# Half of wq on 120 partitions: two hardware loads of the query weights become pieces on GpSimd's queue, ScalarE's queue and SP's queue

## The chip, the cores and the metric

The kernel runs on one core of one Trainium2 chip. The metric is the device time of one execution in microseconds (us), taken as a median over runs. Before the change it is 1324.21 us (three runs, 1323.97 to 1324.29).

## What is computed

The reference is one decode step for two batch rows: a pre-LayerNorm attention block over a long cache, then an MLP. B = 2, D = 512, H = 32 heads of DH = 128, a cache of SK = 8192 positions, all in float32.

```python
h  = x + attention(layernorm(x))
h2 = h + mlp(layernorm(h))            # 512 -> 1792 -> 512, with gelu

def attention(x):
    q = (x @ wq).reshape(B, 1, H, DH)                 # wq: 512 x 4096
    scores = einsum("bhqd,bhkd->bhqk", q, k_cache) * DH ** -0.5
    o = einsum("bhqk,bhkd->bhqd", softmax(scores), v_cache)
    return o.reshape(B, 1, H * DH) @ wo
```

The two caches are 64 tiles each of 8192 x 128 floats, 4 MB (4096 KB in the profile) a tile; together they are nearly all of the 561 MB that the kernel reads. wq is 8 MB.

## The kernel before

**Tiles.** One pair (head h, batch row b) has one key tile and one value tile, 128 partitions of 32 KB. The 64 pairs run in order of h, then b. All these tiles, the two tiles of wq at the start and the MLP weights at the end rotate through one pool, `kv`, of five buffers (`BUFS = 5`, L42). A second pool, `wts`, has two buffers for the 1 MB groups of wo (`load_wo`, L55). A load is issued on SP's queue (`nc.sync.dma_start`) and waits there, ahead of all later loads, until the buffer that it takes is free.

**Start.** x comes in on ScalarE's queue (L49). wq comes in as two tiles of 4 MB on SP's queue (L61 to L66): partition p holds the rows 4p to 4p+3 of wq, two of them in each tile. VectorE and ScalarE compute the layer norm of x (L100 to L109; the Sqrt on ScalarE at L105 is `lnsd`), TensorE transposes it row group by row group (L113, tile `ypt`, copied to `yT` at L115), and 32 matrix instructions (L124) multiply it with wq, into the accumulators `so2`. ScalarE copies the sums to `q2` (L128), and `make_q` (L132) spreads two heads' worth of q over 128 partitions (`qps`, L136).

**Loop.** For pair i (L265), in two halves c of 32 positions per partition: VectorE multiplies the key tile with q in place (`multiply`, L161), sums most of the products (`by_dve`, L170) while ScalarE sums ten positions of each half (`by_act`, L166), takes the maximum over the row (`row_max`, L177), and with both batch rows of a head done the softmax follows (`all_max`, L184; `exps`, L194). The value tile of pair i-2 is multiplied on TensorE (`values`, L215). A key tile is free when VectorE and ScalarE are through with it, a value tile when TensorE is. I write k0, k1, ... and v0, v1, ... for the key and value tiles of pairs 0, 1, ...

**Order.** The loop asks at pair i for the key tile of pair i+1 and then the value tile of pair i-1 (L270, L278); the wo groups come at every eighth pair (L271) and the biases b1 and b2 at pair 56 (L279). The framework's scheduler then fixes the order in each queue, and it gives each DMA of the hardware queues (SP's and ScalarE's together) one of eight completion semaphores in turn; a DMA that takes a semaphore again waits until the DMA before it on that semaphore has landed. GpSimd's DMAs have eight semaphores of their own, used in the same way.

**End.** The last value tile comes in three pieces (L314), then w1 and w2 in ten pieces (L315 to L321). The MLP follows, and the output leaves on two queues (L420).

Of the kernel before, what the change touches and what calls it, by code (L numbers as in the profile page):

```python
# [9 lines left out]
F32 = mybir.dt.float32  # L10
BF16 = mybir.dt.bfloat16
AF = mybir.ActivationFunctionType
ALU = mybir.AluOpType
AX = mybir.AxisListType

P = 128
# [11 lines left out]
def tile_decode_block(ctx: ExitStack, tc: tile.TileContext, x, k, v, wq, wo, w1, b1, w2, b2, out):  # L28
    nc = tc.nc
    B, H, SK, DH = k.shape  # L30
    D = x.shape[-1]
# [3 lines left out]
    DC = D // P  # L35
# [4 lines left out]
    const = ctx.enter_context(tc.tile_pool(name="const", bufs=1))  # L40
    wts = ctx.enter_context(tc.tile_pool(name="wts", bufs=2))
    kv = ctx.enter_context(tc.tile_pool(name="kv", bufs=BUFS))  # L42
    work = ctx.enter_context(tc.tile_pool(name="work", bufs=3))
    psq = ctx.enter_context(tc.tile_pool(name="psq", bufs=2, space=bass.MemoryType.PSUM))
    psm = ctx.enter_context(tc.tile_pool(name="psm", bufs=3, space=bass.MemoryType.PSUM))
    psa = ctx.enter_context(tc.tile_pool(name="psa", bufs=1, space=bass.MemoryType.PSUM))

    x2 = const.tile([B, D], F32, name="x2")
# [9 lines left out]
        nc.sync.dma_start(t, rows.rearrange("(h p) n -> p h n" if g == LG else "(p h) n -> p h n", p=P))  # L58
        wo_g[g] = t

    wqv = wq.rearrange("(p r) n -> p r n", r=DC)  # L61
    wqs = []
    for r in range(0, DC, 2):
        t = kv.tile([P, 2, H * DH], F32, name="wqs", tag="kv")
        nc.sync.dma_start(t, wqv[:, r:r + 2, :])  # L65
        wqs += [t[:, 0, :], t[:, 1, :]]  # L66

    ident = const.tile([P, P], F32, name="ident")
    make_identity(nc, ident)
    epst = const.tile([P, 1], F32, name="epst")  # L70
    nc.vector.memset(epst, EPS)
    eps2 = const.tile([P, 1], F32, name="eps2")
# [23 lines left out]
    so2 = [psa.tile([P, 512], F32, name=f"so{j}") for j in range(2)]  # L96
# [5 lines left out]
    mv = work.tile([B, 2], F32, name="lnmv")  # L102
# [2 lines left out]
    nc.scalar.activation(sd, mv[:, 1:2], AF.Sqrt, bias=epst[:B])  # L105
    rs = work.tile([B, 1], F32, name="lnrs")
    nc.vector.reciprocal(rs, sd)
    y2 = const.tile([B, D], F32, name="y2")
    nc.vector.tensor_scalar(y2, x2, mv[:, 0:1], rs, op0=ALU.subtract, op1=ALU.mult)  # L109

    ypt = psm.tile([P, DC, B], F32, name="sm")
    for r in range(DC):
        nc.tensor.transpose(ypt[:, r, :], y2.rearrange("b (p r) -> b r p", r=DC)[:, r, :], ident[:B, :B])  # L113
    yT = const.tile([P, DC, B], F32, name="yT")
    nc.vector.tensor_copy(yT, ypt)  # L115
    pick = const.tile([P, B, P], F32, name="pick")
    nc.vector.tensor_copy(pick, sel_all[:, :B, None].to_broadcast([P, B, P]))

    QW = H * DH // NG
    q2 = const.tile([P, QW], F32, name="q2")  # L120
    for r in range(DC):
        for j in range(QW // 512):
            for n in range(NG):
                nc.tensor.matmul(so2[j][32 * n:32 * n + B], yT[:, r, :],  # L124
                                 wqs[r][:, n * QW + j * 512:n * QW + (j + 1) * 512],
                                 start=(r == 0), stop=(r == DC - 1))
    for j in range(QW // 512):
        nc.scalar.activation(q2[:, j * 512:(j + 1) * 512], so2[j], AF.Copy)  # L128

# [135 lines left out]
    for i in range(NP):  # L265
        h, b = pairs[i]
# [94 lines left out]
    with behind(last):  # L361
        for n in range(NG):
            last = nc.tensor.matmul(po2[32 * n:32 * n + 32], ident[:B, :32], resb[:, n * P:(n + 1) * P],
                                    start=True, stop=False)
# [10 lines left out]
    for c in range(DC):  # L375
        last = nc.tensor.matmul(acc[:, c, :], wlc.rearrange("d (p c) -> d c p", c=DC)[:, c, :], OT[hl],
                                start=True, stop=True)
    with behind(last):
        for n in range(NG):
            nc.tensor.matmul(po2[32 * n:32 * n + B], OT[hl], wl[:, n * P:(n + 1) * P],  # L380
                             start=False, stop=False)
# [8 lines left out]
    for c in range(DC):  # L390
        for n in range(NG):
            last = nc.tensor.matmul(
                pf[32 * n:32 * n + B], cen[:, c, :], w1t[:, c, n * FN:(n + 1) * FN],
                start=(c == 0), stop=(c == DC - 1))
# [18 lines left out]
    for t in range(FT):  # L413
        for n in range(NG):
            nc.tensor.matmul(po2[32 * n:32 * n + B], fT[:, t, :B], w2t[:, t, n * P:(n + 1) * P],
                             start=False, stop=(t == FT - 1))
# [29 lines left out]
```

## Time and profile before

| | |
|---|---|
| median of three runs | 1324.21 us |
| the profiled execution | 1324.32 us |
| its span, first to last instruction | 1322.5 us |
| VectorE busy | 989.5 us, 75% of the span |
| TensorE matmuls busy | 530.4 us, 40% |
| ScalarE busy | 442.0 us, 33% |
| GpSimd busy | 1.3 us |
| read from HBM | 561.01 MB, 424 GB/s over the span |
| packets of SP's and ScalarE's data queues | 22300, 98.9% of 16 engines' span |
| instruction queues q8 and q14 | 23 packets, 0.38 MB and 29 packets, 0.24 MB |
| median from issue to landing, key tile and value tile | 42.9 us and 34.4 us |

How to read it: the core has 16 DMA engines, and a load of 128 partitions puts 8 partitions on each of them. The DMA share is the mean over the 16. A load counts as landed when all the engines it uses have added to its semaphore; the trace records each of these additions and each packet. "PEclk" is the clock that TensorE was granted, as a part of full speed. In the chain of waits DMA has 73% of the span, VectorE 18% and TensorE 7%.

### The profile page before, as it was taken

How to read it: one execution, taken by the hardware profiler on the slowest of the kernel's cores; microseconds unless marked ns; L12 is line 12 of the kernel's file. 1: busy time of each engine (PE TensorE's matmuls, PEld its weight loads, DVE VectorE, ACT ScalarE, POOL GpSimd, SP SyncE). 2: the span in 40 equal slices, each digit the busy share in tenths (PEclk: the TensorE clock that was granted, in tenths of full speed). 3: DMA queues.
4: the chain of work that ended last, by engine and by line, in shares of the span. 5: the costliest groups of instructions: out<-in, count | busy, mean ns of one | idle time of the engine just before them, and what ended most of it. 6: DMA issues, size and time to landing. Idle time of an engine off the chain costs nothing.

```text
span 1322.5 us, 9641 instructions
## 1 busy us (share of the span) xinstructions
PE 530.4 (40%) x2901; PEld 143.3 (11%) x2901; DVE 989.5 (75%) x459; ACT 442.0 (33%) x2763; POOL 1.3 (0%) x10
## 2 busy tenths in 40 slices
PE   4044234334244244434336244263343532444347
PEld 1011001101011011100101011010011100011013
DVE  1997877867877778868778778777778768687781
ACT  0433323324323324324323333323333333243241
POOL 0000000000000000000000000000000000000000
PEclk9566666666676676676676666676766766666668
DMA  9999999999999999999999999999999999999995
GB/s 412 427 429 429 436 431 429 427 432 434 432 428 430 434 431 431 430 429 432 434 429 431 431 432 430 433 429 432 430 431 432 431 431 428 432 429 431 428 424 216
DMA packets 22364, 561.64 MB, mean 425 GB/s; under 512 B 2452, under 2 KB 2468, under 8 KB 4136
## 3 DMA queue, kind: packets, MB, share of 16 engines
q1 hardware_dynamic: 22300, 561.02, 98.9%
q8 instruction: 23, 0.38, 0.1%
q14 instruction: 29, 0.24, 0.0%
q10 hardware_dynamic: 12, 0.01, 0.0%
HBM read 561.01 MB, written 0.00 MB: 424 GB/s over the span
## 4 chain that ended last, share of the span: by engine, by line
DMA 73%; DVE 18%; PE 7%; issue 1%; ACT 0%; SPq 0%; DVEq 0%
DMA kv<-in_A_k_cache_dram 51%; DMA kv<-in_A_v_cache_dram 19%; DVE kv L161 12%; PE so L215 6%; DVE s L170 5%; DMA w1s<-in_B_w_dram 3%; DMA w2s<-in_B_w_dram 1%; PE qps L136 1%; DVE gm L184 0%; ACT kv L166 0%; DVE orow L242 0%; ACT L194 0%; DVE mx L177 0%; SPq L152 0%; SPq L65 0%
## 5 line engine op out<-in xcount | busy, mean ns | idle before, releaser
L161 DVE TENSOR_TENSOR kv<-kv,qps 128x4096 f32<-128x4096 f32 x128 | 562.3, 4413 | 286.3 <-DMA kv<-in_A_k_cache_dram 286.3
L166 ACT ACTIVATE kv<-kv 128x128 f32<-128x128 f32 x1280 | 376.0, 295 | 687.0 <-DVE kv L161 670.9
L215 PE MATMUL so<-kv,pt 128*8 128x512 f32 x2048 | 374.2, 855 | 258.6 <-DMA kv<-in_A_v_cache_dram 256.2
L170 DVE TENSOR_REDUCE s<-kv 128x22 f32<-128x2816 f32 x128 | 390.9, 3075 | 0.1
L166 ACT ACTIVATION_READ_ACCUMULATOR kv<-kv 128x1 f32 x1280 | 238.7, 187 | 0.0
L215 PEld LDWEIGHTS so<-kv,pt 128*8 128x8 f32 x2048 | 63.3, 113 | 500.2 <-DMA kv<-in_A_v_cache_dram 249.8
L186 PE MATMUL sm<-gm,srow 1*128 1x2 f32 x64 | 18.1, 349 | 192.1 <-DVE gm L184 192.1
L136 PE MATMUL qps<-q,pick 2*128 2x256 f32 x64 | 30.8, 631 | 135.7 <-DVE kv L161 135.7
L222 ACT ACTIVATE ss<-so 128x512 f32<-128x512 f32 x32 | 19.1, 597 | 148.4 <-PE so L215 148.4
L180 PE MATMUL sm<-ident,mx 128*1 128x128 f32 x64 | 17.7, 276 | 66.4 <-DVE mx L177 61.3
L254 PE MATMUL rowacc<-wog,ot 128*2 128x512 f32 x56 | 38.5, 852 | 5.2 <-DVE ot L252 5.0
L186 PEld LDWEIGHTS sm<-gm,srow 1*128 1x128 f32 x64 | 15.5, 299 | 204.2 <-DVE gm L184 160.7
L203 PE MATMUL sm<-ones,ls 128*2 128x1 f32 x56 | 5.4, 165 | 76.2 <-ACT pt L194 76.2
L232 PE MATMUL sm<-ss,sel 128*2 128x128 f32 x224 | 29.0, 273 | 13.3 <-ACT ss L222 13.1
L136 PEld LDWEIGHTS qps<-q,pick 2*128 2x128 f32 x64 | 17.5, 299 | 142.2 <-DVE kv L161 138.5
L194 ACT ACTIVATE pt<-s,nb 128x64 f32<-128x64 f32 x64 | 21.7, 340 | 1.1
L232 PEld LDWEIGHTS sm<-ss,sel 128*2 128x2 f32 x224 | 16.7, 84 | 23.5 <-ACT ss L222 19.4
L177 DVE TENSOR_REDUCE mx<-s 128x1 f32<-128x64 f32 x64 | 14.1, 220 | 6.5 <-ACT kv L166 0.2
L180 PEld LDWEIGHTS sm<-ident,mx 128*1 128x1 f32 x64 | 5.1, 79 | 122.9 <-DVE mx L177 77.0
L124 PE MATMUL so<-wqs,yT 128*2 128x512 f32 x64 | 10.8, 834 | 11.4 <-DMA wqs<-in_A_wq_dram 11.4
L184 DVE TENSOR_REDUCE gm<-sm 1x2 f32<-1x256 f32 x32 | 12.8, 401 | 0.5 <-PE sm L180 0.5
L237 DVE TENSOR_TENSOR ot<-sm,rl 128x2 f32<-128x2 f32 x4 | 0.6, 156 | 15.4 <-PE sm L230 15.4
(85 smaller groups left out, 109.6 us busy)
## 6 DMA issues: line engine op xcount, KB each, us to landing
kv<-in_A_k_cache_dram SPq DMA_DIRECT2D x63, 4096.0 KB, 42.9
kv<-in_A_v_cache_dram SPq DMA_DIRECT2D x62, 4096.0 KB, 34.4
wqs<-in_A_wq_dram SPq DMA_DIRECT2D x2, 4096.0 KB, 16.7
wog<-in_A_wo_dram SPq DMA_DIRECT2D x8, 1024.0 KB, 45.3
kv<-in_A_v_cache_dram SPq DMA_DIRECT2D x3, 2048.0 KB
kv<-in_A_k_cache_dram SPq DMA_DIRECT2D x2, 2048.0 KB, 40.1
w1s<-in_B_w_dram SPq DMA_DIRECT2D x4, 896.0 KB, 34.1
w2s<-in_B_w_dram SPq DMA_DIRECT2D x2, 1024.0 KB
```

What stands on the lines that cost most here:

```text
L136: nc.tensor.matmul(t[:, b], pick[32 * n:32 * n + B, b, :], q2[32 * n:32 * n + B, at:at + QG * DH], start=True, stop=True)
L161: return nc.vector.tensor_tensor(kc, kc, qb, op=ALU.mult)
L166: nc.scalar.activation(kt[:, j, :], kt[:, j, :], AF.Copy, accum_out=s[:, j:j + 1])
L170: nc.vector.tensor_reduce(ST[i][:, a:e], kt[:, a:e, :], axis=AX.X, op=ALU.add)
L177: nc.vector.tensor_reduce(MX[h][:, b:b + 1], ST[i], axis=AX.X, op=ALU.max)
L180: nc.tensor.transpose(MT[h][:, e, :], MX[h][:, e:e + 1], ident)
L186: nc.tensor.matmul(GM[h], srow, gm, start=True, stop=True)
L194: nc.scalar.activation(ptz[h % 2][b][:, :, 4 * b:4 * b + 4], s.rearrange("p (u j) -> p u j", j=4), AF.Exp, bias=nb[:, b:b + 1], scale=SCAL ...
L215: m = nc.tensor.matmul(so[32 * n:32 * n + 4 * B], ptz[h % 2][b][:, u, :], vt[:, 4 * u:4 * u + 4, :], start=(b == 0 and u < NG), stop=(b == ...
L222: nc.scalar.activation(SS[h], so2[h % 2], AF.Copy)
L232: nc.tensor.matmul(OP[h], sel[:, :, j], sj, start=(j == 0), stop=(j == 3))
L254: nc.tensor.matmul(rowacc, t[:, r, :], wo_g[g][:, r, :], start=(g == 0 and r == 0), stop=False)
```

## The change

wq has 512 rows. Rows 0 to 239 go into one tile, `wqa`, two rows to a partition, on 120 partitions; partitions 4 to 7 and 36 to 39 stay zero. Rows 240 to 495 go into a second tile, `wqb`, two rows on each of 128 partitions, in one load on SP's queue. The last 16 rows go on every eighth partition of two tiles of half a row each, `wqc`, which take the two buffers of the wo pool.

`wqa` comes in by 24 DMAs on GpSimd's queue and 8 on ScalarE's. On GpSimd's queue eight groups follow each other, their order held by `issue_after`: a filler of 2 elements of b1, a piece of 6 rows of 32 KB to partitions with a stride of 4, and a piece of 8 rows likewise. The 8 DMAs on ScalarE's queue carry one partition of 32 KB each, to partitions 0 to 3 and 32 to 35; they stand ahead of the Sqrt of the layer norm there.

VectorE and GpSimd first zero half of partitions 0 to 39 of `wqa` each (40 x 4096 elements), and VectorE zeroes both `wqc` tiles (128 x 2048 each). The DMAs into these tiles wait for that. The layer norm's result is written in five pieces instead of one, into a zeroed tile with gaps at the eight empty partitions; there are five transposes instead of four. The matrix instructions go over `wqb`, then `wqa`, then `wqc`: 16, 16 and 8 instead of 32.

In the order that the scheduler makes of it, on SP's queue: b2 (one row), `wqb`, the two `wqc`, k0, k1, k2, b1 (twice), b2, v0, k3, the first two wo groups, v1, k4, v2, k5, v3, and on as before. Before it is: the two wq tiles, k0, k1, k2, v0, k3, v1, k4, the first wo group, v2, k5, v3. b1 and b2 were loaded at pair 56.

```diff
--- before.py
+++ after.py
@@ -58,15 +58,48 @@
         nc.sync.dma_start(t, rows.rearrange("(h p) n -> p h n" if g == LG else "(p h) n -> p h n", p=P))
         wo_g[g] = t
 
-    wqv = wq.rearrange("(p r) n -> p r n", r=DC)
-    wqs = []
-    for r in range(0, DC, 2):
-        t = kv.tile([P, 2, H * DH], F32, name="wqs", tag="kv")
-        nc.sync.dma_start(t, wqv[:, r:r + 2, :])
-        wqs += [t[:, 0, :], t[:, 1, :]]
-
+
+
+    VOID = (4, 36)
+    NA = 2 * (P - 4 * len(VOID))
+    wqa = kv.tile([P, 2, H * DH], F32, name="wqs", tag="kv")
+    nc.vector.memset(wqa[0:40, 0], 0.0)
+    nc.gpsimd.memset(wqa[0:40, 1], 0.0)
     ident = const.tile([P, P], F32, name="ident")
     make_identity(nc, ident)
+    fill = const.tile([2, 8], F32, name="fill")
+    turns = iter(range(8))
+    rows = wq[0:NA].rearrange("(q r) n -> q r n", r=2)
+
+    pool = nc.gpsimd.memset(fill, 0.0)
+
+    def in_turn(dst, src):
+        nonlocal pool
+        with tc.issue_after(pool.ins):
+            pool = nc.gpsimd.dma_start(dst, src)
+
+    def turn_to(n):
+        e = next(turns)
+        in_turn(fill[:n, e:e + 1], b1[:, None][:n])
+
+    def spread(p0, q0, n):
+        in_turn(wqa[p0:p0 + 4 * n - 3:4], rows[q0:q0 + 4 * n - 3:4])
+
+    for half in range(2):
+        for j in range(4):
+            turn_to(2)
+            spread(32 * half + 8 + j, 28 * half + 4 + j, 6)
+            spread(64 + 32 * half + j, 56 + 32 * half + j, 8)
+    for half in range(2):
+        for j in range(4):
+            nc.scalar.dma_start(wqa[32 * half + j:32 * half + j + 1], rows[28 * half + j:28 * half + j + 1])
+    wqb = kv.tile([P, 2, H * DH], F32, name="wqs", tag="kv")
+    nc.sync.dma_start(wqb, wq[NA:NA + 2 * P].rearrange("(p r) n -> p r n", r=2))
+    wqc = [wts.tile([P, H * DH // 2], F32, name="wqc", tag="wog") for _ in range(2)]
+    for j in range(2):
+        nc.vector.memset(wqc[j], 0.0)
+        nc.sync.dma_start(wqc[j][::8], wq[NA + 2 * P:D, j * H * DH // 2:(j + 1) * H * DH // 2])
+
     epst = const.tile([P, 1], F32, name="epst")
     nc.vector.memset(epst, EPS)
     eps2 = const.tile([P, 1], F32, name="eps2")
@@ -105,25 +138,39 @@
     nc.scalar.activation(sd, mv[:, 1:2], AF.Sqrt, bias=epst[:B])
     rs = work.tile([B, 1], F32, name="lnrs")
     nc.vector.reciprocal(rs, sd)
-    y2 = const.tile([B, D], F32, name="y2")
-    nc.vector.tensor_scalar(y2, x2, mv[:, 0:1], rs, op0=ALU.subtract, op1=ALU.mult)
-
-    ypt = psm.tile([P, DC, B], F32, name="sm")
-    for r in range(DC):
-        nc.tensor.transpose(ypt[:, r, :], y2.rearrange("b (p r) -> b r p", r=DC)[:, r, :], ident[:B, :B])
-    yT = const.tile([P, DC, B], F32, name="yT")
+    y2 = const.tile([B, DC + 1, P], F32, name="y2")
+    nc.vector.memset(y2, 0.0)
+
+    def rows_of(r0, n, p0, p1, d0):
+        nc.vector.tensor_scalar(y2[:, r0:r0 + n, p0:p1],
+                                x2[:, d0:d0 + n * (p1 - p0)].rearrange("b (p r) -> b r p", r=n),
+                                mv[:, 0:1], rs, op0=ALU.subtract, op1=ALU.mult)
+
+    rows_of(0, 2, 0, 4, 0)
+    rows_of(0, 2, 8, 36, 8)
+    rows_of(0, 2, 40, P, 64)
+    rows_of(2, 2, 0, P, NA)
+    nc.vector.tensor_scalar(y2[:, 4, ::8], x2[:, NA + 2 * P:D], mv[:, 0:1], rs, op0=ALU.subtract, op1=ALU.mult)
+    ypt = psm.tile([P, DC + 1, B], F32, name="sm")
+    for r in range(DC + 1):
+        nc.tensor.transpose(ypt[:, r, :], y2[:, r, :], ident[:B, :B])
+    yT = const.tile([P, DC + 1, B], F32, name="yT")
     nc.vector.tensor_copy(yT, ypt)
     pick = const.tile([P, B, P], F32, name="pick")
     nc.vector.tensor_copy(pick, sel_all[:, :B, None].to_broadcast([P, B, P]))
 
     QW = H * DH // NG
     q2 = const.tile([P, QW], F32, name="q2")
-    for r in range(DC):
+    for r in (2, 3, 0, 1, 4):
         for j in range(QW // 512):
             for n in range(NG):
-                nc.tensor.matmul(so2[j][32 * n:32 * n + B], yT[:, r, :],
-                                 wqs[r][:, n * QW + j * 512:n * QW + (j + 1) * 512],
-                                 start=(r == 0), stop=(r == DC - 1))
+                at = n * QW + j * 512
+                if r == 4:
+                    w = wqc[at // (H * DH // 2)][:, at % (H * DH // 2):]
+                else:
+                    w = (wqa, wqb)[r // 2][:, r % 2, at:]
+                nc.tensor.matmul(so2[j][32 * n:32 * n + B], yT[:, r, :], w[:, :512],
+                                 start=(r == 2), stop=(r == 4))
     for j in range(QW // 512):
         nc.scalar.activation(q2[:, j * 512:(j + 1) * 512], so2[j], AF.Copy)
 
```

## The prediction

> **What bounds the kernel now.** I read the busy time by stage first, then the chain of work that ended last, then the SP queue's timeline, then the start instruction by instruction. By stage (columns: length, then busy time of PE, weight loads, VectorE, ScalarE, GpSimd, granted clock, DMA share, GB/s):
>
> ```profile
> core 0: us, PE busy (x) PEld busy (x) DVE busy (x) ACT busy (x) POOL busy (x), PEclk, DMA share, GB/s
> 1.70:33.00 31.30, 13.28 (x76) 3.87 (x76) 4.27 (x15) 2.41 (x4) 0.13 (x1) 0.90 1.03 433
> 33.00:82.00 49.00, 6.45 (x34) 2.35 (x38) 46.85 (x18) 20.41 (x126) 0.00 (x0) 0.50 1.00 428
> 82.00:110.00 28.00, 16.73 (x93) 4.31 (x85) 27.79 (x13) 13.54 (x86) 0.00 (x0) 0.76 1.01 431
> ...
> 1308.50:1318.00 9.50, 7.30 (x135) 3.19 (x127) 1.49 (x3) 2.71 (x4) 0.00 (x0) 0.90 0.07 28
> ```
>
> From 1.7 us on the DMA engines are full at about 430 GB/s, whoever the chain names. The last row carries the idea of the change: for 9.5 us only 0.07 of 16 engines works, 28 GB/s, one sixteenth. One engine finishes 10 us after the other fifteen. The landing records agree: the last of the 16 semaphore increments of a load comes 0.03 us after the last but one at 32 us, 1.7 at 293, 8.5 at 1050, 10.2 at the end. The steady growth fits the instruction queue q8 on the page: 22 of its 23 packets of 16 KB come after 81 us, and half of a 32 KB packet (1.214 us in the packet records) is 0.6 us, so 13 us in all. The end goes by that engine, which never idles before it. Two things can move the time: work taken off it, or a stretch in which it is empty.
>
> **What is taken off.** [...] The profiled execution is 1324.32, the median of the runs 1324.21; I add to the first.
>
> **What the start costs.** The start before:
>
> ```profile
> 3.89 0.29 ACT L105 ACTIVATE lnsd<-lnmv,epst 2x1 f32<-2x1 f32 x1 [1.27 <-DVE lnmv L103]
> 5.73 0.17 DVE L115 COPY yT<-sm 128x8 f32<-128x8 f32 x1 [0.51 <-PE sm L113]
> 12.94 5.44 PE L124 MATMUL so<-wqs,yT 128*2 128x512 f32 x32 [7.24 <-DMA wqs<-in_A_wq_dram]
> 22.56 5.31 PE L124 MATMUL so<-wqs,yT 128*2 128x512 f32 x32 [4.18 <-DMA wqs<-in_A_wq_dram]
> 27.80 1.99 PE L136 MATMUL qps<-q,pick 2*128 2x256 f32 x8
> 32.33 4.42 DVE L161 TENSOR_TENSOR kv<-kv,qps 128x4096 f32<-128x4096 f32 x1 [25.82 <-DMA kv<-in_A_k_cache_dram]
> ```
>
> The layer norm is done at 5.9 us, q waits only for wq, and the first multiply starts at 32.33 with the first key load k0. The changed kernel, built but not run, shows the waits of each instruction, and three decide:
>
> (1) ScalarE issues eight row DMAs ahead of the Sqrt of the layer norm (lnsd). Hardware-queue DMAs share eight semaphores in turn, and the seventh waits on semaphore 1 for the value that the second key load k1 brings. So layer norm, q and every multiply wait until k1 has landed. Before, k1 lands at 41.94 as fourth load of 4 MB (landings 12.80, 22.51, 32.23, 41.94: 9.71 each). Now wqb, k0, k1 and the rows of wqa are as many bytes; plus 0.6 for wqc and 0.45 for one more SP issue ahead (two take 0.87): 43.0. If none of wqa's rows were served by then it would be 33.3. I take 43.0, as GpSimd's DMAs start at about 7 us: its 40x4096 memset is 32 times the 128-column one (three in 0.49 us), 5.2.
>
> From k1 to the first multiply: wake-up 0.1; two ScalarE issues 0.9 (between SP's 0.33 and the 0.56 of x); table load 1.28; Sqrt to yT 2.0 as above, and 0.45 for four more VectorE pieces, one more transpose and the hand-over; 16 matmuls on wqb 5.44, 16 on wqa 5.31, 8 on wqc half of that, 2.7; qps 2.1. Sum 20.3: the first multiply at 63.3, 31 us later than before. The memsets of VectorE (4096 columns at 0.43 us for 448 is 3.9; two of 2048, 3.9 together), the split layer norm and ident all lie in that wait and cost nothing more.
>
> (2) SP's first value load v0 waits for semaphore 3, the landing of k2 (52.7), and for wqb's matmuls (43.0 + 4.7 + 5.44 = 53.1). Until then nothing is queued on SP. Issue to first packet took 1.02 us (0.73 to 1.75), so it begins at 54.2. An engine without rows of wqa is through with k2 at 43.0 and stands empty for 11.2 us. **That is the whole lead, spent at once.**
>
> (3) Then buffers come free only as VectorE goes on. Before:
>
> ```profile
> 0.73 0.87 SPq L65 DMA_DIRECT2D wqs<-in_A_wq_dram  x2
> ...
> 47.15 0.33 SPq L152 DMA_DIRECT2D kv<-in_A_v_cache_dram  x1
> 66.24 0.33 SPq L152 DMA_DIRECT2D kv<-in_A_k_cache_dram  x1
> 66.61 0.43 SPq L58 DMA_DIRECT2D wog<-in_A_wo_dram  x1
> 79.23 0.33 SPq L152 DMA_DIRECT2D kv<-in_A_v_cache_dram  x1
> 83.00 0.33 SPq L152 DMA_DIRECT2D kv<-in_A_k_cache_dram  x1
> ```
>
> These are v1, k4, wo, v2, k5, each behind the tile whose buffer it takes: 14.8, 33.9, 46.9 and 50.7 us after the first multiply. k4 was issued some 15 us before the engines ran out, so a delay of 31 cannot be hidden. Now: v0 54.2 to 63.9, k3 (behind wqa's matmuls, 58.5) to 73.6, both wo loads (wqc shares their buffers, so SP now has them here) 2.43 each to 78.5; v1 issued at 63.3 + 14.8 = 78.1, packets from 79.1 to 88.8. k4 is issued at 97.2, packets at 98.2: all sixteen idle 9.4 us. Before, its packets began at 82.1 (landed 91.84). 98.2 - 82.1 = 16.1, less 4.9 for the two wo loads that came later before: 11.2 us lost. k4 is through at 107.9, v2 is issued at 110.2, packets at 111.2: 3.3 lost. A restart: the first packets of the run took some 0.65 us over 1.214; two of them, between 0 and 1.3, I take 0.6. Then k5 (issued 114.0, queue until 121) and v3 (63.9 after the multiply, 127.2, queue until 131) come in time, and VectorE (7.5 us of multiply and reduce per half tile, 15 per key, against 19.4 of DMA per key and value) runs ahead of the queue again. Sum: 11.2 + 3.3 + 0.6 = 15.1. Nothing gives it back, since DMA is full later in both. b1 and b2, moved to the start, and the eight fillers are under 20 KB: nothing.
>
> **Forecast: 1324.3 + 15.1 = 1339.4 us, slower.** Since every engine is empty ahead of k4, it hardly matters whose rows were left out.
>
> **Unknown: GpSimd's DMAs.** The trace has none. wqa is late only if it lands after 53.1: at 7 us of start and 2.5 of service, 24 issues of up to 1.8 us are hidden. Ends: SP's 0.33 below; above no row, so I try 2.5. [...]
>
> **Rivals.**
> Slow GpSimd queue: at 2.5 us per issue wqa lands at 69.5, the first multiply comes at 79.6, 16 later: about 1356. Against it: eight may be in flight, and each piece is two to eight rows.
> Pieces on the wrong engines: every piece starts on the first engine, so the pieces of 6 and 8 rows heap 16 rows on engines 0 to 5. Eight more rows ahead of k1 are 9.7 us: 1349. No row speaks on it. [...]
> [...]
> The change misses the late engine: b1's four-row loads show it is one of the few engines such a load uses (one of four packets comes 14 us late), but no row numbers it. Then there is no gain even without the waits; time as in the forecast.
>
> **Chances.** Forecast (1332 to 1345; its lower end is k1 at 36 with wqa in time) 0.74; pieces on the wrong engines 0.09; slow queue 0.10; lead kept 0.04; the delays cancel within 0.2% 0.03. A measurement of this kernel cannot tell less than 0.2% from no change. Faster 0.04, same 0.03, slower 0.93. The range, 1332 to 1351, takes in the wrong engines and leaves out the slow queue's far end and the faster case.
>
> **What would show it.** lnsd right behind the landing of k1 (near 44 us), the first multiply near 63, no packets on the freed engine near 43 to 54, DMA share well under 1 near 89 to 98 and 108 to 111, one engine still last by about 10 us at the end. Wrong if the multiply starts by 50 or DMA is full between 50 and 110.

## The result and the profile after

The changed kernel takes **1381.89 us** (median of four runs, 1380.88 to 1383.73), the kernel before 1324.12 (1323.97 to 1324.29) beside it: a ratio of 1.0438, 95% interval 1.042 to 1.0456. The profiled execution took 1382.77, its span is 1381.0. The forecast was 1339.4; it is 42.5 us too low.

The first view is the page's slices, each 1/40 of the span, 34.5 us (share of the DMA engines in tenths, then GB/s):

```profile
DMA  9856999999999999999999999999999999999995
GB/s 296 249 200 289 376 428 429 433 428 435 428 434 430 427 433 430 430 434 427 432 431 429 432 431 432 429 430 432 429 431 431 430 429 428 433 429 430 429 425 231
```

All of the loss is in the first five slices, some 170 us. From the sixth on the two kernels read the same. The next view is busy time by stage, the same stages as before the change and one row between 11 and 29 us (columns as in the prediction):

```profile
1.70:33.00 31.30, 0.00 (x0) 0.00 (x0) 10.66 (x21) 0.00 (x0) 9.91 (x18) 1.00 1.02 315
33.00:82.00 49.00, 5.86 (x37) 1.49 (x37) 1.63 (x7) 1.58 (x2) 6.21 (x14) 1.00 0.72 218
82.00:110.00 28.00, 9.15 (x56) 2.72 (x56) 5.56 (x2) 2.29 (x10) 0.00 (x0) 0.64 0.72 277
1366.00:1376.50 10.50, 8.17 (x134) 3.34 (x127) 1.49 (x3) 2.71 (x4) 0.00 (x0) 0.82 0.12 43
```

```profile
11.00:29.00 18.00, 0.00 (x0) 0.00 (x0) 2.26 (x10) 0.00 (x0) 2.07 (x4) 1.00 1.01 249
```

The kernel before, in the same stretch:

```profile
11.00:29.00 18.00, 11.88 (x70) 2.96 (x71) 0.00 (x0) 1.19 (x2) 0.00 (x0) 0.91 1.01 435
```

Three things are to be seen. In the row from 11 to 29 us the DMA engines are full (share 1.01) and yet move 249 GB/s instead of 435: each packet takes longer (SP's of 32 KB 2.17 us instead of 1.213, medians from 12 to 30 us). From 33 us on they are also idle (0.72). And at the end one engine still works alone: the last addition to a load's semaphore comes 9.1 us after the last but one (10.2 before).

The start, in time order on ScalarE, VectorE and TensorE:

```profile
5.22 64.00 ACTq L95 DMA_DIRECT2D wqs<-in_A_wq_dram  x8
69.25 1.28 ACT L138 ACT_TABLE_LOAD   x1 [69.25 <-DMA wqs<-in_A_wq_dram]
70.55 0.29 ACT L138 ACTIVATE lnsd<-lnmv,epst 2x1 f32<-2x1 f32 x1
```

```profile
72.73 0.17 DVE L158 COPY yT<-sm 128x10 f32<-128x10 f32 x1 [0.36 <-PE sm L156]
104.44 8.75 DVE L208 TENSOR_TENSOR kv<-kv,qps 128x4096 f32<-128x4096 f32 x2 [31.55 <-PE qps L183]
```

```profile
72.95 5.16 PE L172 MATMUL so<-wqs,yT 128*2 128x512 f32 x32 [0.26 <-DVE yT L158]
96.12 5.52 PE L172 MATMUL so<-wqs,yT 128*2 128x512 f32 x32 [18.01 <-DMA wqs<-in_A_wq_dram]
```

The layer norm waits behind ScalarE's rows as forecast, but until 70.55 instead of 44. It does not decide: the matrix instructions on `wqb` are over at 78.1, and those on `wqa` begin at 96.12. The first multiply is at 104.44 instead of 63.3. The chain of waits names what they wait for (start, length, what):

```profile
8.54 40.44 DMA wqs<-in_A_wq_dram
48.98 0.28 issue
49.26 31.37 DMA fill<-in_B_b_dram
80.63 0.28 issue
80.91 14.40 DMA wqs<-in_A_wq_dram
95.31 0.81 issue
96.12 7.24 PE so L172 x48
```

Three DMAs of GpSimd's queue one behind another, 86.2 us. GpSimd's own timeline shows how the second came to be issued at 49.26 (the bracket is the idle time ahead of it and what ended it):

```profile
8.54 0.52 POOL L79 DMA_DIRECT2D wqs<-in_A_wq_dram  x1
12.74 0.52 POOL L79 DMA_DIRECT2D wqs<-in_A_wq_dram  x1 [3.68 <-DMA fill<-in_B_b_dram]
21.64 0.52 POOL L79 DMA_DIRECT2D fill<-in_B_b_dram  x1 [8.38 <-DMA wqs<-in_A_wq_dram]
...
49.26 0.52 POOL L79 DMA_DIRECT2D fill<-in_B_b_dram  x1 [4.97 <-DMA wqs<-in_A_wq_dram]
...
80.91 0.52 POOL L79 DMA_DIRECT2D wqs<-in_A_wq_dram  x1 [3.27 <-DMA fill<-in_B_b_dram]
```

An issue takes 0.52 us. But GpSimd's 24 DMAs take turns on eight semaphores (three on each in the landing records), so from the ninth on each waits for a landing (the ninth goes out at 12.74, the first landed at 12.46), and a piece lands 27 to 30 us after its issue (medians of the page: 30.4 for eight rows, 27.3 for six, 27.9 for a filler of eight bytes). A load that carries 8 bytes and takes as long as one of 256 KB is not slowed by its own bytes.

The packet records put a size on both effects. I add them up over the first 165 us, as a mean of the 16 engines: time that packets took beyond 1.214 us per 32 KB, 23.3 us against 1.2 before; time with no packet, 37.4 against 1.5. Together 58.0 us more; the span grew by 58.5. So, by this account, **22 us of the loss are slow packets and 36 are empty engines.**

### The profile page after: what moved, and what is told of

Same layout as the page of the kernel before. It is cut to its first block, busy times and chain, and to the rows that moved or that the text cites. A ratio compares the mean times of both kernels' runs of the same rounds, so it can differ in the third digit from the quotient of the medians.

```text
span 1381.0 us, 9743 instructions
## 1 busy us (share of the span) xinstructions
PE 533.1 (39%) x2917; PEld 145.0 (10%) x2918; DVE 997.0 (72%) x467; ACT 442.1 (32%) x2763; POOL 17.3 (1%) x36
## 4 chain that ended last, share of the span: by engine, by line
DMA 74%; DVE 17%; PE 8%; issue 1%; POOL 0%; SPq 0%; ACT 0%; DVEq 0%; ACTq 0%; POOLq 0%
DMA kv<-in_A_k_cache_dram 46%; DMA kv<-in_A_v_cache_dram 18%; DVE kv L208 11%; PE so L262 6%; DVE s L217 5%; DMA wqs<-in_A_wq_dram 4%; DMA w1s<-in_B_w_dram 2%; DMA fill<-in_B_b_dram 2%; PE qps L183 1%; DMA w2s<-in_B_w_dram 1%; PE so L172 1%; DVE gm L231 0%; POOL wqs L79 0%; POOL fill L79 0%; DVE orow L289 0%
## 5 line engine op out<-in xcount | busy, mean ns | idle before, releaser
L301 PE MATMUL rowacc<-wog,ot 128*2 128x512 f32 x56 | 37.4, 830 | 5.2 <-DVE ot L299 5.1
## 6 DMA issues: line engine op xcount, KB each, us to landing
wqs<-in_A_wq_dram POOLq DMA_DIRECT2D x8, 256.0 KB, 30.4
```

The costliest lines, as they stand in the source:

```text
L301: nc.tensor.matmul(rowacc, t[:, r, :], wo_g[g][:, r, :], start=(g == 0 and r == 0), stop=False)
```

## The experiments

Times without an interval are of one run; runs of the kernel before beside them gave 1323.97 to 1324.61. "Landing" is that of the last piece of `wqa` (or of the tile that stands for it).

| run | landing | first multiply | time |
|---|---|---|---|
| before | 22.5 | 32.33 | 1324.12 |
| after (profiled execution) | 95.31 | 104.44 | 1382.77 |
| rows_behind | 102.56 | 111.59 | 1390.30 |
| whole_pool | 25.21 | 35.82 | 1324.41 |
| eight_low | 34.88 | 44.31 | 1328.74 |
| eight_high | 44.52 | 52.57 | 1338.04 |
| one_piece | 25.59 | 34.20 | 1327.45 |
| no_fillers | 90.96 | 100.65 | 1378.97 |
| sixteens_sp | 23.57 | 42.89 | 1334.76 |
| pieces_sp | 46.04 | 56.20 | 1348.02 |
| no_wqa | - | 27.55 | 1317.38 |
| low_2 | 34.15 | 42.13 | 1328.29 |
| engine0 | 34.07 | 44.26 | 1325.27 |
| sixteens | 45.20 | 54.79 | 1335.60 |
| heap_low | 61.22 | 70.34 | 1348.93 |
| heap_high | 79.64 | 88.17 | 1366.76 |

**Is it ScalarE's order? (rows_behind)** The eight row DMAs stand behind the Sqrt.

```diff
+    root = nc.scalar.activation(sd, mv[:, 1:2], AF.Sqrt, bias=epst[:B])
...
+            with tc.issue_after(root.ins):
+                nc.scalar.dma_start(wqa[32 * half + j:32 * half + j + 1], rows[28 * half + j:28 * half + j + 1])
```

> The changed kernel with its eight ScalarE row DMAs behind the Sqrt of the layer norm instead of ahead of it. If the ScalarE order was what delayed the first multiply (104.4 us), it comes with the landing of wqa no longer mattering and the time falls by tens of us, to about 1340. If the landing of wqa by GpSimd's queue (95.3 us) is what ends last, lnsd comes near 13 us instead of 70.6, yet the first multiply stays within some 5 us of 104 and the time between 1372 and 1384 us.

Measured 1390.3: the Sqrt ran at 13.23 us, and the first multiply came at 111.59, since the last piece landed at 102.56. The order on ScalarE, step (1) of the forecast, is a real wait that another one covers. The time missed the expectation upwards. In this run v0 goes out at 28.01 instead of 86.52, so SP's queue has packets for longer while the pieces are under way; that would make them land later, but no run shows it alone.

**Is it GpSimd's queue as such? (whole_pool)** The kernel before, with its first wq tile as one load of 128 partitions on that queue.

```diff
-        nc.sync.dma_start(t, wqv[:, r:r + 2, :])
+        (nc.gpsimd if r == 0 else nc.sync).dma_start(t, wqv[:, r:r + 2, :])
```

> The kernel before with the first of its two wq tiles issued as one load of 128 partitions on GpSimd's queue; nothing else of the change. If GpSimd's queue beside a full SP queue slows all packets whatever it carries, packets of 32 KB take over 2 us while it is in flight, the tile lands after 40 us and the time rises by 10 us or more. If the trouble lies in the pieces (how many there are, which engines and partitions they join), packets stay near 1.21 us, the tile lands by about 25 us and the time is 1322 to 1328 us.

Measured 1324.41, ratio 1.0002 (0.9993 to 1.0012). Packets stay at 1.213 us. The queue alone, with one load on it, costs nothing.

**Is it the rest of the change? (one_piece)** The changed kernel, with `wqa` in one load.

```diff
-    for half in range(2):
-        for j in range(4):
-            turn_to(2)
-            spread(32 * half + 8 + j, 28 * half + 4 + j, 6)
-            spread(64 + 32 * half + j, 56 + 32 * half + j, 8)
...
+    in_turn(wqa, wq[0:2 * P].rearrange("(p r) n -> p r n", r=2))
```

> The changed kernel with the sixteen pieces, the fillers and ScalarE's eight rows replaced by one load of 128 partitions on GpSimd's queue (rows 0 to 255 of wq; the layer norm uses partitions 0 to 119 of it). wqb, wqc, the zeroing, the five transposes and the 40 matrix instructions stay. Theory (the small pieces are the whole loss: engines 0 to 5 carry 16 rows each, every row and every semaphore write of GpSimd's queue waits for a packet of SP's, and packets that cross partitions take twice as long): the tile lands near 30 us, the first multiply is near 42, 32 KB packets stay at 1.21 us, 1324 to 1331 us. Rival (the rest of the change, with the value load v0 behind the matrix instructions of wqb and the wo loads moved forward, costs by itself what was forecast): 1335 to 1340 us.

Measured 1327.45, ratio 1.0025 (1.0015 to 1.0035). Its stages, to be held beside those of the changed kernel:

```profile
1.70:33.00 31.30, 13.26 (x93) 4.15 (x93) 11.90 (x26) 2.40 (x4) 4.33 (x9) 1.00 1.00 411
33.00:82.00 49.00, 4.57 (x22) 1.62 (x26) 45.66 (x18) 20.40 (x126) 0.00 (x0) 0.51 1.01 432
```

So the small pieces (the rows on ScalarE's queue among them) are 54 of the 58 us. The tile landed earlier than expected, at 25.59, and then the waits of step (2) leave no stall behind: the engines are full from 33 us on.

**On which engines do the pieces lie, and what do they wait for? (eight_low, eight_high)** Only eight pieces of 8 rows, with no fillers and no rows on ScalarE, into the lower or the upper 64 partitions.

```diff
-            turn_to(2)
-            spread(32 * half + 8 + j, 28 * half + 4 + j, 6)
-            spread(64 + 32 * half + j, 56 + 32 * half + j, 8)
+            spread(0 + 32 * half + j, 56 + 32 * half + j, 8)    # eight_high: 64 for 0
...
```

> The changed kernel with eight pieces of 8 rows alone on GpSimd's queue, into partitions 0 to 63 with a stride of 4; no fillers, no pieces of 6, no ScalarE rows; all of wqa is zeroed first and the rest of it is not loaded, so q lacks nearly half of the rows of wq. Theory of crossed partitions: a piece's rows go to engines 0 to 7 in turn, here each to the engine that serves those partitions in full loads, so 32 KB packets stay near 1.21 us (median under 1.35) while the pieces are in flight, wqa lands by 40 us, time 1320 to 1332. Theory that GpSimd's queue slows every engine: median over 2 us as in the changed kernel, same as the run into partitions 64 to 127.

> [...] Theory of crossed partitions: the rows are carried by engines 0 to 7 into partitions that engines 8 to 15 write at the same time, so packets slow to about 2.2 us while the pieces are in flight, wqa lands 15 us or more later than in the run into partitions 0 to 63, and the time is 1335 us or more. Theory that GpSimd's queue slows every engine whatever it carries: the same packet time and the same time as the other run within 3 us.

Measured 1328.74 and 1338.04, both in the range of the theory of crossed partitions; eight_high's tile landed 9.6 us after eight_low's, where 15 or more were expected. In eight_low the last four landings are 3.64 us apart (23.96, 27.59, 31.24, 34.88), one piece at a time, and the packet records show the same eight engines with a row of each piece and the other eight with none. One engine with rows, in time order:

```
24.31 GpSimd row 1.22 | 25.52 SP packet 1.22 | 26.73 GpSimd semaphore 0.01 | 26.74 SP packet 1.22 | 27.95 GpSimd row 1.22 | 29.17 SP packet ...
```

Here the engine takes its two queues in turn, packet by packet. The 4-byte write that ends a piece waits for a whole 32 KB packet of SP's (1.22 us), like the row itself. So here a row costs three packet times, 3.65 us, as long as SP's queue is full. The stages of the two runs show the difference between the partitions, eight_low first:

```profile
11.00:23.00 12.00, 5.80 (x37) 1.52 (x37) 3.89 (x17) 0.29 (x1) 0.00 (x0) 1.00 0.99 374
23.00:35.00 12.00, 0.00 (x0) 0.01 (x1) 0.00 (x0) 0.00 (x0) 0.00 (x0) 0.67 1.01 434
```

```profile
11.00:23.00 12.00, 4.44 (x25) 1.38 (x29) 3.89 (x17) 0.29 (x1) 0.00 (x0) 1.00 0.96 240
23.00:35.00 12.00, 2.11 (x16) 0.24 (x8) 0.00 (x0) 0.00 (x0) 0.00 (x0) 0.68 0.99 311
```

Same DMAs, same engines, full share in both; 434 GB/s where the eight engines with rows write partitions 0 to 63, 311 where they write 64 to 127. GpSimd's rows take 1.22 and 2.23 us (medians). I call the slow case *crossing* and read it as an engine writing partitions that another engine serves in a load of 128. That is an inference from the two rates; whose partitions are whose, engine by engine, no run shows, and the expectations of the later runs take the reading as given. A *heap* is several rows one behind another on the same few engines.

**What does a crossed partition cost without GpSimd? (sixteens_sp, sixteens)** The kernel before, its first wq tile in eight pieces of 16 partitions, on SP's queue and on GpSimd's.

```diff
+        if r == 0:
+            for j in range(8):
+                nc.sync.dma_start(t[j::8], wqv[j::8, r:r + 2, :])    # sixteens: nc.gpsimd
```

> [...] No GpSimd DMA. Theory (crossed partitions halve the packets' pace: two engines on the partitions of one): the eight pieces take 2.43 us per packet instead of 1.21, the first multiply comes 9.7 us later, 1334 us. Rival (a packet's time does not depend on the partition it is written to): 1324 to 1326 us, packets of 1.21 us.

> The kernel before, with the first wq tile in the eight pieces of 16 partitions of stride 8, on GpSimd's queue: eight rows on every engine, no heap, but partitions crossed (two engines on one's partitions) and GpSimd's turns (a row and a semaphore write, each behind a packet of SP's). Theory: 8 rows x 3 packets x 1.2 to 1.6 us: the tile lands between 33 and 43 us, the first multiply is between 42 and 52, 1327 to 1336 us. Rival (many DMAs on GpSimd's queue beside a full SP queue are enough for most of the loss, with no heap): landing after 60 us, over 1345 us.

sixteens_sp: 1334.76 (theory 1334). Packets of the pieces took 2.54 us (median), and the stage of the pieces reads

```profile
5.00:23.00 18.00, 0.61 (x4) 0.55 (x4) 0.89 (x6) 0.00 (x0) 0.00 (x0) 1.00 0.96 208
23.00:35.00 12.00, 7.40 (x48) 1.42 (x52) 0.00 (x0) 0.00 (x0) 0.00 (x0) 0.97 1.00 431
```

Sixteen engines at work (share 0.96), half the bytes (208 GB/s): as if two wrote into the partitions of one. That is the theory's reading; the rate is what was measured. sixteens landed at 45.20 and took 1335.6: the time was in its range, landing and multiply 2 to 3 us past theirs (some 5.1 us per piece). With no heap, turns and crossing together cost 11.3 us (1324.29 beside it).

**Do the fillers matter? (no_fillers)** The changed kernel without `turn_to(2)`.

> The changed kernel without the eight fillers: sixteen DMAs on GpSimd's queue instead of 24. Theory (every piece starts on the first engine whatever goes before it; a filler only costs one semaphore write, and so one turn behind a packet of SP's, on every engine): on the six engines with 16 rows a group costs four packets of SP's and two rows instead of five and two, 6/7 of the 81 us between 14 and 95 us, so the last piece lands near 84 us and the time is near 1370 us. Rival 1 (the rows alone set the pace): no change, 1380 to 1384 us. Rival 2 (a cursor turns on from piece to piece, and the fillers steer it): the rows now start on other engines than before, spread over all sixteen, and the time falls under 1355 us or the landings lose their order.

Measured 1378.97, 2.9 less; the last piece landed at 90.96. They neither steer the pieces nor cost much. The time lies between the theory's 1370 and the rival's 1380: the landing came 4.4 us earlier, not 11. Why a filler costs less than its turn is not shown.

**What is left on SP's queue? (pieces_sp)** The sixteen pieces on SP's queue behind `wqb`, no fillers, ScalarE's rows behind the Sqrt.

```diff
-            pool = nc.gpsimd.dma_start(dst, src)
+            pool = nc.sync.dma_start(dst, src)
```

> The changed kernel with the same sixteen pieces on SP's queue, right behind wqb, without fillers, and ScalarE's eight rows behind the Sqrt. The rows fall on the same engines 0 to 5 and 6 to 7 and cross partitions as before; what goes is the turns between GpSimd's queue and SP's. Theory (the three costs multiply: heap of 16 rows, packets of double length, and two packets of SP's per row): without the turns the 16 rows take 16 x 2 = 32 us behind wqb's 11, so the last piece lands at 40 to 50 us, the first multiply at 50 to 60, and the time is 1340 to 1352 us. Rival (the pieces themselves, not the queue, set the landing): the last piece lands after 80 us and the time stays over 1370 us.

Measured 1348.02, landing at 46.04 and first multiply at 56.20, all within the ranges, but with another loss than I had in mind:

```profile
11.00:23.00 12.00, 7.08 (x37) 1.64 (x37) 3.88 (x17) 0.29 (x1) 0.00 (x0) 1.00 0.48 199
23.00:35.00 12.00, 0.00 (x0) 0.00 (x0) 0.00 (x0) 0.00 (x0) 0.00 (x0) 0.57 0.26 93
```

The queue itself runs dry (share 0.26). I put it down to the eight semaphores that SP's and ScalarE's DMAs share (eight in the landing records, before and after the change), which 16 more DMAs now take in turn, so that key loads wait for pieces to land. The trace fits: most pieces from the fifth on go out behind a landing, the last at 35.16, and the first key load behind them at 37.21 (9.97 in the changed kernel). No run tried that alone.

**Heap and crossing at full size (heap_low, heap_high)** Sixteen pieces of 8 rows, twice over the same 64 partitions: 16 rows each for the eight engines that carry pieces.

```diff
+    for again in range(2):
...
+                spread(0 + 32 * half + j, 56 * again + 32 * half + j, 8)    # heap_high: 64 for 0
```

> The changed kernel with sixteen pieces of 8 rows on GpSimd's queue, all into partitions 0 to 63 (the second eight over the first; rows of other partitions, ScalarE's rows and the fillers are left out): the first eight engines have 16 rows each as in the changed kernel, with a row and a semaphore write each behind a packet of SP's, but each engine writes the partitions that it serves in a whole load. Theory (heap and turns without crossing): packets stay at 1.22 us, the first 13 rows take 3.65 us each as in the run with eight such pieces, the last three 1.2 (SP's 26 packets are used up): the last piece lands at 62 to 70 us, the first multiply at 72 to 80, time 1348 to 1362 us. Rival (heap and turns alone explain the result): last landing after 85 us, time over 1372 us.

> The same sixteen pieces into partitions 64 to 127: same engines, same turns, but every row goes to partitions that another engine serves. Theory (crossing is the third part): 5 us per row while SP's queue is full, as with eight such pieces, the last piece lands at 80 to 92 us, the first multiply at 90 to 102, time 1368 to 1384 us. Rival (no matter at 16 rows): within 3 us of the run into partitions 0 to 63.

Measured 1348.93 and 1366.76. In heap_low, packets stay at 1.22 us and pieces land 3.65 us apart up to 61.22; in heap_high GpSimd's rows take 2.20 us and the landing is at 79.64, both a little ahead of the expectation; heap_high's time is 1.2 us under its range, heap_low's within it. The chains of waits, heap_low first:

```profile
9.14 25.32 DMA wqs<-in_A_wq_dram
34.46 0.28 issue
34.74 26.48 DMA wqs<-in_A_wq_dram
61.22 0.14 issue
```

```profile
9.14 36.00 DMA wqs<-in_A_wq_dram
45.14 0.28 issue
45.42 34.22 DMA wqs<-in_A_wq_dram
79.64 0.14 issue
```

**Is the late engine the one that is left out? (no_wqa, low_2, engine0)** `wqa` only zeroed; then eight two-row pieces (engines one and two get eight rows each, if a piece starts where those of eight_low do); then one DMA of 17 half rows, a count with no divisor up to 16.

```diff
+            spread(0 + 32 * half + j, 56 + 32 * half + j, 2)                 # low_2, instead of 8
+    nc.sync.dma_start(wqa[64:97:2, 0], rows[64:97:2, 0])                     # engine0
```

> The changed kernel with wqa zeroed and not loaded at all (it leaves out rows 0 to 239 of wq): every engine has 8 rows of 32 KB less than in the kernel before. It is the base of the next two runs. Where the end goes by the late engine, the best that leaving out a whole tile can give is 9.7 us: 1314.5, plus the 3.3 us that the rest of the change cost in the run with one whole piece: 1314 to 1319 us.

> The run without wqa, and eight pieces of 2 rows on GpSimd's queue into partitions 0-7 and 32-39: by what the runs have shown, the first two engines get eight rows each and nobody else any (it leaves out the other 224 rows of wq). If the late engine is one of these two, the time is that of the run without wqa plus 9.7 us (with the same number above for the first engine alone, run engine0). If it is a later engine, the same as the run without wqa, within 1 us.

> The run without wqa, and one DMA of 17 half rows (17 x 16 KB = 8.5 rows) on SP's queue behind wqb, a count that no number of engines from 2 to 16 divides, into partitions 64 to 96 in steps of 2 (it leaves out nearly all of rows 0 to 239 of wq). Theory: it lies on the first engine alone. If the late engine is the second (the change's premise), the first one's slack of 10 us takes the 10.3 us and the time is that of the run without wqa, within 1 us, while the run with two-row pieces is 9.7 us longer. If the first engine is the late one, 10.3 us more here too.

Measured 1317.38, 1328.29 (+10.9) and 1325.27 (+7.9; expected +0 to 1, or +10.3). In engine0 the 17 packets of 16 KB follow one another on one engine and take 1.2 us each on average, not 0.61 (the median of SP's 16 KB packets before): 20.3 us, not 10.3. I put that down to crossing. Its landing records near the end show two late engines, one 7.2 us behind the rest and one 2.4 behind that; in no_wqa there is one, by 10.0. So the engine of the 17 rows was not the late one. In low_2 the last engine is 15.6 us behind the next: the late one did get rows. By both together, if the 17 rows lay on the engine where the pieces start, the late engine is the second, the one that the change, by its premise, spares. Loads stalled in both runs (DMA share 0.38 from 75 to 80 us in engine0, 0.55 from 85 to 90 in low_2), so the times alone would not have told it.

## Why the prediction was wrong

**The sum by experiments.** Each line is the difference of two runs: 3.3 the rest of the change (one_piece); 1.3 eight rows on eight engines, in partitions 0 to 63 (eight_low); 20.2 sixteen rows instead of eight (heap_low); 17.8 the crossing (heap_high); 15.1 from there to the change as it is, of which the fillers are 2.9 (no_fillers). Together 57.7. The parts are those of this order of runs: eight_low loads 2 MB less than one_piece and heap_low, which load as much as each other.

**Bound, late engine, direction: right, the direction in part by luck.** The end still goes by one engine (9.1 us behind the others). That the partitions left empty are those of the late engine is the change's premise; no run shows it. That the instruction queue q8 makes it late is not shown: q8's packets took 1.08 us (median), not half of 1.214, and the one at 1308.98 in the kernel before ran while the late engine's packets followed each other without a gap. Slower came true by a wait that the sum had at nothing, the landing of `wqa`. Whether wait (1) alone would have cost 15.1 us was not tried: one_piece has no rows ahead of the Sqrt.

**Step (3), from the first multiply to the end: right.** v1, k4 and v2 were forecast 14.8, 33.9 and 46.9 us after the first multiply. SP's issues after the change:

```profile
86.52 0.34 SPq L199 DMA_DIRECT2D kv<-in_A_v_cache_dram  x1
101.75 0.33 SPq L199 DMA_DIRECT2D kv<-in_A_k_cache_dram  x1
103.39 0.85 SPq L58 DMA_DIRECT2D wog<-in_A_wo_dram  x2
119.25 0.33 SPq L199 DMA_DIRECT2D kv<-in_A_v_cache_dram  x1
138.37 0.33 SPq L199 DMA_DIRECT2D kv<-in_A_k_cache_dram  x1
151.35 0.33 SPq L199 DMA_DIRECT2D kv<-in_A_v_cache_dram  x1
```

That is 14.8, 33.9 and 46.9 behind 104.44. Time minus first multiply is 1278.3 in the changed kernel, 1278.3 in no_fillers, 1278.7 in rows_behind, 1278.6 in heap_low and heap_high; the forecast had 1276.1. Where the multiply starts before 57 us, the multiply alone no longer sets the time (pieces_sp 1291.8, eight_high 1285.5).

**Step (1): the wait is there, its size was wrong.** I took k1 at 43.0. Eight engines had added to its semaphore by 45.58, the other eight only between 52.56 and 68.67: as many as carry pieces. ScalarE's seventh row went out at 68.69, right behind. And it did not decide (rows_behind).

**Step (2): as said, but much longer.** v0 went out at 86.52, right behind the landing of k2 (86.44), not at 53.2.

**The step that failed: "wqa is late only if it lands after 53.1: at 7 us of start and 2.5 of service, 24 issues of up to 1.8 us are hidden."** I priced GpSimd's DMAs by what an issue takes. That was even generous (0.52 us, start at 4.84). The price lies in the landing: three packet times per row (3.65 us in eight_low), 16 rows on an engine, rows that take 1.9 us (median) and up to 2.6. `wqa` landed at 95.31. The first multiply was 41.1 us late on the forecast, and the time 42.5.

**The rival "pieces on the wrong engines" had the mechanism and not the price.** For pieces of 8 rows the runs show it: they land one at a time, 3.64 us apart, each with a row on the same eight engines (eight_low). Pieces of 2 rows fit it (low_2: the last engine 15.6 us behind, against 10.0 in no_wqa). I gave it eight more rows at 1.214, 9.7 us. Eight more rows cost 20.2, as each waits for two packets of SP's; and the same rows into partitions 64 to 127 cost 17.8 more (heap_high), which I put down to crossing. That its time, 1349, is that of heap_low (1348.93) is luck: it was 9.7 on top of the forecast's 15.1 from steps (1) to (3), and heap_low has no rows ahead of the Sqrt, so no wait of step (1).

**Left open.** The 12.2 us between heap_high and the change without fillers (six-row pieces, ScalarE's eight rows); neither was tried alone. Of the 3.3 us of the rest, 1.9 are there when the third 4 MB tile lands (34.10 against 32.23); where the others arise is not shown. No version beat the kernel before: the gain that no_wqa shows, 6.9 us, is that of not loading 4 MB, and every piece of two or more rows that was tried, but for the odd count of engine0, put rows on the late engine too.

## What to carry to other kernels

Price a DMA beside a full queue by its landing, not its issue: in eight_low each row and each completion write waited for a 32 KB packet of the other queue (1.22 us), and in the changed kernel a load of 8 bytes, behind up to seven others of its own queue, took 28 us. Before cutting a load into pieces, find on which engines they fall, and try whether other partitions take them faster; here a full DMA share at half the GB/s (208 instead of 431 in sixteens_sp) was the sign of what I call crossing. When one late event gates a pipeline, check the steps behind it by their distance from that event: those held here within 3 us, and nearly the whole error was in the event's time.

## What the runs showed of the hardware that was not expected

- A GpSimd DMA adds to its semaphore 16 times however small it is (48 additions for three DMAs on each of eight semaphores, the changed kernel), which I read as once on each engine: 24 packets of 4 bytes for a piece of 8 rows (eight_low), 26 for 6 (no_fillers), 32 for a filler, its own 2 elements among them (the changed kernel), 16 for a load of 128 partitions (one_piece); on engines with rows, the closing write waited its turn behind a 32 KB packet (1.22 us, eight_low).
- Pieces of every eighth partition, half the rate: 208 GB/s with all 16 engines busy (sixteens_sp), packets of 2.54 us instead of 1.21. Packets of SP's loads of 128 partitions were slowed too (median 2.17 us between 12 and 30 us in the changed kernel).
- From GpSimd's issue to the first packet it took 4.6 us (issue at 5.43, packet at 10.00, one_piece) and 4.9 us (whole_pool, issue at 1.22); the engines were full, so a turn behind a packet of SP's, 1.2 us, can be in it.
- The DMA of 17 half rows lay on one engine: 17 packets one after another, 20.3 us, in engine0.
